# Masked attention and a two-layer MLP on one core: first-layer input sums moved earlier and partly to VectorE, input operands spread over the cycles, leaky ReLU beside attention as a scaled copy and a maximum, weight decoding in halves

## The chip, the core and the metric

The kernel runs on one core of a Trainium2 chip. A core has a matrix engine (TensorE, "PE" in the profile; "PEld" is its weight loading), a vector engine (VectorE, DVE), a scalar engine (ScalarE, ACT), GpSimd (POOL) and a sync engine (SP), which issues the DMAs here. PE results land in PSUM, which DVE and ACT read; everything else lives in SBUF or in DRAM. Every engine works through its own queue in order and waits on semaphores for the others. The metric is the device time in microseconds (us) of one execution; the medians are over three runs.

## The reference, cut to what matters

Attention over 8 batches, 8 heads, 576 positions and 64 columns, with a mask that keeps only scores near the row's maximum, and then a two-layer MLP with a leaky ReLU over all 4608 tokens:

```python
scores = scale * np.matmul(q, k.transpose(0, 1, 3, 2))            # (8, 8, 576, 576)
thresh = np.max(scores, axis=-1, keepdims=True) - tau
scores = np.where(scores >= thresh, scores, -1000000000.0)
attn = np.exp(scores - np.max(scores, axis=-1, keepdims=True))
attn = attn / (np.sum(attn, axis=-1, keepdims=True) + 1e-09)
x = (attn @ v).transpose(0, 2, 1, 3).reshape(4608, 512)
h = x @ w_in                                                      # w_in 512 x 2048
g = np.maximum(h, 0.0) + alpha * np.minimum(h, 0.0)               # one alpha per column
return (g @ w_out).astype(np.float32)                             # w_out 2048 x 512
```

The weights arrive as 64-bit words and are decoded on the chip. Every product keeps its precision by splitting an operand into a rounded high part and the rest ("hi" and "lo": names with h and l) and adding three products.

## The kernel before, in words

**Attention (0 to about 840 us).** The 64 heads are handled in 32 pairs of nine row blocks each: 288 units, one per "cycle" of a written loop that goes on for a few cycles at both ends. In a cycle PE computes the scores of a coming block (`s`, L431) and transposes an earlier block's weights (`t`, L475), DVE takes the row maximum (`nmx`, L446) and applies the mask (`p`, L466), ACT takes the exponential (`p`, L454) and the threshold (`thr`, L459), and both split the transposed weights for the product with v (`av`, L578). Finished tokens go to DRAM as `xs`.

**The MLP beside attention.** Of the 16 blocks of the hidden layer six (`fcs1`) are computed in the plain way, in groups of 256 tokens, beside attention where the loop finds room on PE (class `Mlp`). One "L1 step" is 12 matmuls into `pha` (L218). `step_l1` first reads the group's x back from `xs` (`load_x`, L198), splits it a set number of cycles later (XO; `split_x`, L204 on ACT and L206 on POOL) and lets the first L1 step come two cycles after that. Leaky ReLU follows an L1 step: DVE writes alpha·min(h, 0) (`pta`, L230), ACT writes max(h, 0) (`pra`, L231), POOL adds them (L241), then POOL (or ACT) rounds the sum to `ga` and POOL takes the rest (L247, L248). The second layer (`acca`, L254) comes when all six blocks of the group are there, L2O cycles later at the earliest; HOLD is a stretch of cycles near attention's end in which no L1 step is placed.

**The jobs (about 840 to 930 us).** The last groups of the six blocks run alone as "jobs": `first_layer` (`phj`, L218; leaky ReLU as two DVE instructions, L236 and L237; `gj`, L245 and L248) and `second_layer` (`accj`, L254; its sum leaves through ACT as `poj`, L1089). In between come the weights of the next stage (`w`, `wa`, L866, L869, L995 to L1008).

**Products a (about 930 to 1195 us).** The other ten blocks use seven products in place of eight for a 2 x 2 blocking (a Strassen-Winograd scheme), first for the first layer: six sets of 768 tokens, for each of which four quarters of x (`xr`, loaded by L1131) give seven operands. Four of these are sums: 7 = 11 − 01, 6 = 7 + 00, 4 = 10 − 6 and 5 = 01 − 00 (the digits name the quarters), `tt` at L1136 on DVE for set 0 and at L1139 on POOL, in two halves, for sets 1 to 5. Each operand is split into hi (ACT, L866) and lo (POOL, or DVE for a few of set 0, L869). The products are `pX`, `pW`, `pY` (L1252); ACT copies them out scaled (`c`, L1269, L1277) and DVE joins them (L1280, L1292). PE may start a product on a bank when the copy of the bank's last one is done. `x_at` places every sum, hi and lo of a set at a cycle counted from the product that first needs it (`need`).

**Products b (about 1195 to 1420 us)** do the same for the second layer (L1430), with PE busy throughout.

**Word decoding.** `Split64` turns 512 columns of 64-bit words into floats in seven steps on ACT, DVE and POOL. For the second-stage blocks' first-layer weights this is done early, beside attention (`early_word`, one block every EW = 20 cycles).

**What sets the order.** The instructions of PE, ACT, DVE and POOL stand in the order in which the loop writes them; `at_cycle` puts a step into a cycle. The order of the DMAs on SP's queue is set by a scheduler.

Of the kernel before, what the change touches and what calls it, by code (L numbers as in the profile page):

```python
# [37 lines left out]
HOLD = (-16, -1)  # L38
# [16 lines left out]
XO = 1  # L55
L2O = 3
# [10 lines left out]
EW0, EW = 62, 20  # L67
# [14 lines left out]
def tile_masked_attention_moe(  # L82
# [34 lines left out]
    class Split64:  # L117


        def __init__(self, pool, raw, temp_pool, temp, eng, src, a, name, split=False):  # L120
            self.split = split
            self.pool, self.raw_tag, self.temp_pool, self.temp_tag = pool, raw, temp_pool, temp
            self.eng = [nc.vector if e == 'v' else nc.gpsimd for e in eng]
            self.src, self.a, self.name = src, a, name
# [1409 lines left out]
```

## Time and profile before

| | us |
| --- | --- |
| median of 3 runs (lowest to highest) | 1418.66 (1417.18 to 1421.1) |
| profiled execution | 1421.49 |
| its span, first to last instruction | 1419.6 |
| PE busy (matmuls) | 1320.9, 93% |
| DVE / ACT / POOL busy | 1126.5 (79%) / 967.7 (68%) / 761.7 (54%) |

An engine's busy time is counted over the whole span, so the share is an average over stages with different limits. "Idle before" is the time in which the engine stood still before an instruction or a group of them, and the name behind the arrow is what released it. PEclk is the share of full clock that was granted to PE: 1.0 is 2.4 GHz, 0.5 is 1.2 GHz, and a value between them is a mixture over the stretch.

### The profile page before, as it was taken

The numbers are of one execution on the slowest core, as the hardware profiler recorded it, in microseconds if no ns is written. First come the engines' busy times: TensorE is split into PE (matmuls) and PEld (weight loads), VectorE is DVE, ScalarE is ACT, GpSimd is POOL, SyncE is SP. The second block draws the span as 40 slices with busy tenths as digits, with TensorE's granted clock in tenths as the row PEclk, the third lists the DMA queues.
The fourth block names the chain that finished last, engine by engine and source line by source line (L and its number), as shares of the span: only waits on it lengthen the run. The fifth ranks groups of instructions, "written<-read, shape, count | busy, mean of one in ns | idle before, by whom it ended". The sixth has DMA issues, their size and how long they took to land.

```text
span 1419.6 us, 26277 instructions
## 1 busy us (share of the span) xinstructions
PE 1320.9 (93%) x8998; PEld 1226.8 (86%) x8998; DVE 1126.5 (79%) x2113; ACT 967.7 (68%) x2109; POOL 761.7 (54%) x938
## 2 busy tenths in 40 slices
PE   5998989989989998999999988988899999999998
PEld 4666889989888888998989977978889999999998
DVE  6898898998988988888898874556667558787885
ACT  6887888888878877888888863455656565333332
POOL 3775675774765766676675636646766664000000
PEclk9999999999999999999999999999999999999999
DMA  7655546545555464455545404335444466556542
GB/s 230 168 136 146 148 127 163 153 131 156 148 142 144 127 166 130 132 156 142 160 117 152 119 34 136 103 125 163 160 156 158 134 201 198 179 178 200 182 154 74
DMA packets 146166, 210.32 MB, mean 148 GB/s; under 512 B 16016, under 2 KB 89008, under 8 KB 146032
## 3 DMA queue, kind: packets, MB, share of 16 engines
q1 hardware_dynamic: 146032, 208.63, 50.1%
q8 instruction: 72, 1.18, 0.3%
q14 instruction: 62, 0.51, 0.1%
HBM read 111.75 MB, written 54.67 MB: 117 GB/s over the span
## 4 chain that ended last, share of the span: by engine, by line
PE 56%; issue 11%; DVE 10%; POOL 10%; ACT 8%; DMA 3%; SPq 1%; POOLq 0%; DVEq 0%; ACTq 0%
PE av L578 9%; PE pX L1430 9%; PE s L431 8%; PE acca L254 6%; PE t L475 5%; PE pha L218 5%; PE pW L1430 5%; POOL xl L869 3%; PE pY L1430 2%; DVE p L466 2%; DVE nmx L446 2%; PE pX L1252 2%; POOL xt L1139 2%; PE phj L218 2%; ACT p L454 1%
## 5 line engine op out<-in xcount | busy, mean ns | idle before, releaser
L446 DVE TENSOR_REDUCE nmx<-s 128x1 f32<-128x576 f32 x288 | 216.5, 752 | 66.7 <-PE s L431 62.9
L466 DVE SCALAR_TENSOR_TENSOR p<-s,thr,p 128x576 f32<-128x576 f32 x256 | 206.6, 807 | 3.3 <-ACT thr L459 2.8
L431 PE MATMUL s<-kh,qst 128*128 128x288 f32 x640 | 145.7, 317 | 55.2 <-DVE p L466 36.7
L454 ACT ACTIVATE p<-s,nmx 128x576 f32<-128x576 f32 x256 | 190.1, 742 | 9.1 <-DVE nmx L446 8.8
L431 PEld LDWEIGHTS s<-kh,qst 128*128 128x128 f32 x640 | 100.4, 192 | 86.8 <-issue 43.0
L254 PE MATMUL acca<-wo,ga 128*128 128x512 f32 x504 | 158.4, 426 | 0.0
L475 PE MATMUL t<-ident,p 128*128 128x128 f32 x1024 | 156.4, 276 | 1.1 <-DVE p L466 1.1
L1252 PE MATMUL pX<-xh,wa 128*128 128x384 f32 x480 | 139.6, 347 | 17.4 <-ACT c L1269 12.6
L218 PE MATMUL pha<-xh,wi 128*128 128x256 f32 x688 | 140.5, 287 | 5.9 <-ACT pra L231 4.3
L431 PE MATMUL s<-kl,qst 128*128 128x288 f32 x640 | 133.9, 299 | 0.0
L1430 PE MATMUL pX<-wb,gh 128*128 128x256 f32 x720 | 129.7, 282 | 0.0
L475 PEld LDWEIGHTS t<-ident,p 128*128 128x128 f32 x1024 | 127.5, 142 | 1.5 <-DVE p L466 1.3
L218 PEld LDWEIGHTS pha<-xh,wi 128*128 128x128 f32 x688 | 112.0, 189 | 12.4 <-ACT pra L231 6.9
L1430 PEld LDWEIGHTS pX<-wb,gh 128*128 128x128 f32 x720 | 111.6, 191 | 0.0
L1252 PEld LDWEIGHTS pX<-xh,wa 128*128 128x128 f32 x480 | 90.4, 193 | 23.5 <-ACT c L1269 15.8
L866 ACT ACTIVATE gh<-gr 128x1280 fp32r<-128x1280 f32 x45 | 57.4, 1275 | 74.9 <-PE pX L1430 38.9
L578 PE MATMUL av<-eo,vst 128*128 128x322 f32 (+1 forms) x512 | 107.8, 334 | 0.2 <-ACT xb L591 0.2
L531 DVE TENSOR_TENSOR eo<-t,eo 128x512 fp32r<-128x512 f32 (+1 forms) x168 | 97.2, 591 | 9.8 <-ACT eo L527 9.5
L431 PEld LDWEIGHTS s<-kl,qst 128*128 128x128 f32 x640 | 102.8, 192 | 0.0
L1430 PE MATMUL pX<-wb,gl 128*128 128x256 f32 x360 | 101.6, 282 | 0.0
L254 PEld LDWEIGHTS acca<-wo,ga 128*128 128x128 f32 x504 | 89.5, 194 | 11.4 <-DVE e L531 0.3
L218 PE MATMUL pha<-xl,wi 128*128 128x256 f32 x344 | 97.0, 282 | 0.2 <-POOL xl L206 0.2
(213 smaller groups left out, 3855.3 us busy)
## 6 DMA issues: line engine op xcount, KB each, us to landing
gd<-c SPq DMA_DIRECT2D x90, 192.0 KB
gr<-gd SPq DMA_DIRECT2D x24, 640.0 KB
kr<-in_k_dram SPq DMA_DIRECT2D x31, 320.0 KB
rb<-rvd SPq DMA_DIRECT2D x64, 144.0 KB
xs<-xa SPq DMA_DIRECT2D x32, 288.0 KB
pin<-part SPq DMA_DIRECT2D x18, 512.0 KB
out_dram<-pin SPq DMA_DIRECT2D x18, 512.0 KB
vr<-in_v_dram SPq DMA_DIRECT2D x28, 320.0 KB
```

Source lines behind the costliest of these rows:

```text
L218: nc.tensor.matmul(ph[:, :n], w[:, c, :], xx[:, c, :n], start=(c == 0 and ti == 0), stop=(c == NCC - 1 and ti == 2),)
L254: nc.tensor.matmul(acc[:m, :], gg[:, g, o : o + m], w, start=(first and ti == 0), stop=(last and ti == 2))
L431: nc.tensor.matmul(ps[:, h, :288], w, kk[:, a + h * 288 : a + (h + 1) * 288], start=(ki == 0 and i == 0), stop=(ki == 1 and i == n - 1),)
L446: nc.vector.tensor_reduce(self.nmx[:, j : j + 1], self.S[u][0][:, :, :288], axis=AX.XY, op=ALU.max, negate=True)
L454: nc.scalar.activation(pj, ps[:, :, :288], AF.Exp, bias=nmx[:, j : j + 1], scale=1.0)
L466: nc.vector.scalar_tensor_tensor(pj, ps[:, :, :288], thr[:, j : j + 1], pj, op0=ALU.is_ge, op1=ALU.mult, accum_out=self.sm[:, c : c + 1])
L475: nc.tensor.transpose(tb[:, c, :], pt[:, j, j * D + c * P : j * D + (c + 1) * P], ident)
L531: nc.vector.tensor_tensor(dst[1], ps, f(dst[0]), op=ALU.subtract)
L578: nc.tensor.matmul(pa[:m, :n], w, x, start=(part == 0 and c == 0), stop=(part == z.parts[-1] and c == NKC))
L866: nc.scalar.activation(dst, src, AF.Copy)
L1252: nc.tensor.matmul(ph[:, :H1], a, x[:, c], start=(fresh and c == 0 and ti == 0), stop=(c == 1 and ti == 2), skip_group_check=not fresh,)
L1430: nc.tensor.matmul(acc[:, tb * H2 : (tb + 1) * H2], g[:, pr, tb * P : (tb + 1) * P], w, start=(fresh and n == 0 and ti == 0), stop=(n == l ...
```

## The change

- **Leaky ReLU.** Everywhere two instructions in place of three (beside attention) or of two on DVE (jobs): ACT copies h scaled by a per-column value (`turn_sb`) to `pta`, and DVE takes max(h·`slope_sb`, `pta`). POOL's add and the tile `pra` are gone; the tile `pta` has three buffers (two before). For this form the second-layer weights of the six blocks get the column's factor while they are decoded (`size` with `tiny_sb`, and one more ACT copy of `wto` in `round`).
- **x of the MLP beside attention.** x is loaded into the tile `xl` itself, and lo replaces it there; `xr` is gone. XO goes from 1 to 2, L2O from 3 to 1, HOLD from the last 16 to the last 12 cycles.
- **Early word decoding** in halves of 256 columns, one every 10 cycles.
- **Jobs.** The second layer of the job before the last stands between the last job's fifth and sixth first layers, not behind the sixth. The two `poj` copies of the last job stand between the splits of set 0.
- **Sums of x, sets 1 to 5.** Sums 6 and 5 are single DVE instructions of 768 columns; sums 7 and 4 stay on POOL in halves. Loads, sums, hi and lo have cycles of their own (`need` −33; sums −25, −21, −13, −11; hi at −28, −23, −19, −16, −5, −3, −1, in the order 1, 7, 2, 6, 4, 5, 3; lo a cycle behind).

```diff
-HOLD = (-16, -1)
+HOLD = (-12, -1)
-XO = 1
-L2O = 3
+XO = 2
+L2O = 1
-EW0, EW = 62, 20
+EW0, EW = 62, 10
...
-        def round(self, hi):
+        def round(self, hi, turn=None):
             self.hi = hi
+            if turn is not None:
+                nc.scalar.activation(f(self.t), f(self.t), AF.Copy, scale=turn)
             nc.scalar.activation(hi, f(self.t), AF.Copy)
...
     def load_x(pool, t0, n, gn, bufs):
-        xr = pool.tile([P, NCC, gn], F32, tag=f"xr", name=f"xr{gn}_{t0}", bufs=bufs)
+        xl = pool.tile([P, NCC, gn], F32R, tag="xl", name=f"xl{gn}_{t0}", bufs=bufs)
...
-        nc.scalar.activation(xh[:, :, :n], xr[:, :, :n], AF.Copy)
-        xl = pool.tile([P, NCC, gn], F32R, tag="xl", name=f"xl{gn}_{t0}", bufs=bufs)
-        nc.gpsimd.tensor_tensor(xl[:, :, :n], xr[:, :, :n], f(xh[:, :, :n]), op=ALU.subtract)
+        nc.scalar.activation(xh[:, :, :n], f(xl[:, :, :n]), AF.Copy)
+        nc.gpsimd.tensor_tensor(xl[:, :, :n], f(xl[:, :, :n]), f(xh[:, :, :n]), op=ALU.subtract)
...
-        nc.vector.tensor_scalar(t[:, :n], ph[:, :n], 0.0, alpha_sb[:, fc : fc + 1], op0=ALU.min, op1=ALU.mult)
-        nc.scalar.activation(r[:, :n], ph[:, :n], AF.Relu)
-        return t, r
...
-        nc.vector.tensor_scalar(t[:, :n], ph[:, :n], 0.0, alpha_sb[:, fc : fc + 1], op0=ALU.min, op1=ALU.mult)
-        nc.vector.scalar_tensor_tensor(t[:, :n], ph[:, :n], 0.0, t[:, :n], op0=ALU.max, op1=ALU.add)
+        col = slice(fc, fc + 1)
+        nc.scalar.activation(t[:, :n], ph[:, :n], AF.Copy, scale=turn_sb[:, col])
+        nc.vector.scalar_tensor_tensor(
+            t[:, :n], ph[:, :n], slope_sb[:, col], t[:, :n], op0=ALU.mult, op1=ALU.max
+        )
         return t
-
-    def prelu2(t, r, n):
-        nc.gpsimd.tensor_tensor(t[:, :n], t[:, :n], r[:, :n], op=ALU.add)
...
-                if k == 0 and num > 0 and not last and not (num == 1 and pending.begun):
+                if k == (GB - F1 - 1 if last else 0) and num > 0 and not (num == 1 and pending.begun):
                     second_layer(pending, mem.mp1)
...
-            def tt(out, a, b, op):
-                if first:
+            def tt(out, a, b, op, alone=False):
+                if first or alone:
                     nc.vector.tensor_tensor(out, a, b, op=op)
...
-                tt(st[5], st[0, 1], st[0, 0], op=ALU.subtract)
+                tt(st[5], st[0, 1], st[0, 0], ALU.subtract, True)
...
-                tt(temp(6), st[7], st[0, 0], op=ALU.add)
+                tt(temp(6), st[7], st[0, 0], ALU.add, True)
...
-            at_cycle(need[1] - 32, load)
-            for m, n in enumerate(USE):
-                c = need[1] - 22 + 3 * m
-                if m >= XB - 7:
-                    c = max(c, start[u - 1, USE[m + 7 - XB]] + 2)
-                fn = {7: sub7, 6: add6, 4: sub4, 5: sub5}.get(n)
-                if fn:
-                    at_cycle(c - 1, fn)
-                at_cycle(c, hi, n)
-                at_cycle(c + 1, lo, n)
+            at_cycle(max(i, need[1] - 33), load)
+            for c, fn in ((-25, sub7), (-21, add6), (-13, sub5), (-11, sub4)):
+                at_cycle(need[1] + c, fn)
+            for c, n in zip((-27, -22, -18, -15, -4, -2, 0), USE):
+                at_cycle(need[1] + c - 1, hi, n)
+                at_cycle(need[1] + c, lo, n)
...
-        others()
-        for put in puts:
-            put()
+        others(puts)
```

**ACT in attention, around two leaky ReLUs.** These are rows of ACT's queue in the same stretch of one group (the numbers behind the names count tiles). Before:

```order
L231 ACTIVATE pra_3_6826<-pha_3_6786 128x256
L527 ACTIVATE tt_123<-tk_t 64x64
L527 ACTIVATE tt_125<-tk_t 64x64
L527 ACTIVATE eo_117<-t_4_6815 128x4x64 x2
L454 ACTIVATE p_2_6804<-s_6_6808,nmx_5_6801 128x576
L459 ACTIVATE thr_5_6802<-nmx_5_6801,ntau_sb 128x1
L231 ACTIVATE pra_4_6884<-pha_4_6830 128x256
```

and now:

```order
L522 ACTIVATE tt_125<-tk_t 64x64
L522 ACTIVATE eo_117<-t_4_6777 128x4x64 x2
L449 ACTIVATE p_2_6766<-s_6_6770,nmx_5_6763 128x576
L454 ACTIVATE thr_5_6764<-nmx_5_6763,ntau_sb 128x1
L232 ACTIVATE pta_3_6845<-pha_3_6790,turn_sb 128x256
L522 ACTIVATE eo_117<-t_5_6820 128x4x128
L449 ACTIVATE p_3_6852<-s_7_6811,nmx_7_6849 128x576
```

One ACT instruction per leaky ReLU stands there in both; it reads the L1 step's result and nothing of DVE's now, and the L1 steps (blocks 3, 4) lie on other cycles than before.

**ACT at the hand-over from the jobs to products a.** `xh0_n` is the hi of operand n of set 0, `poj3_0` and `poj3_128` are the last job's copies, `c1_0` and `c7_0` the first products' copies. Before:

```order
L866 ACTIVATE xh0_7_12973<-xt0_7_12841 128x768
L866 ACTIVATE xh0_2_12977<-xr0_10_12839 128x768
L866 ACTIVATE xh0_6_12981<-xt0_6_12848 128x768
L866 ACTIVATE xh0_4_12987<-xt0_4_12985 128x768
L866 ACTIVATE xh0_5_12992<-xr0_01_12836 128x768
L866 ACTIVATE xh0_3_12997<-xr0_11_12833 128x768
L1089 ACTIVATE poj3_0_12941<-accj3_0_12922 128x512
L1089 ACTIVATE poj3_128_12961<-accj3_128_12942 128x512
L1269 ACTIVATE c1_0_13035<-pX0_13011,turn_sb_69 128x384
```

and now:

```order
L861 ACTIVATE xh0_7_12920<-xt0_7_12859 128x768
L1081 ACTIVATE poj3_0_12888<-accj3_0_12869 128x512
L861 ACTIVATE xh0_2_12926<-xr0_10_12857 128x768
L1081 ACTIVATE poj3_128_12908<-accj3_128_12889 128x512
L861 ACTIVATE xh0_6_12932<-xt0_6_12866 128x768
L861 ACTIVATE xh0_4_12938<-xt0_4_12936 128x768
L861 ACTIVATE xh0_5_12943<-xr0_01_12854 128x768
L861 ACTIVATE xh0_3_12948<-xr0_11_12851 128x768
L1256 ACTIVATE c1_0_12982<-pX0_12958,turn_sb_69 128x384
```

The two `poj` copies move ahead of five and of four hi's; `c1_0` stays behind all of them.

**POOL in products a, set 1.** `xt1_n` and `xr1_01` on the left of the arrow at L1139 (now L1131) are sums, `xl1_n` are lo's, `wto` and `wro` are words of coming weights. Before:

```order
L1139 TENSOR_TENSOR xt1_7_13157<-xr1_11_13029,xr1_01_13031 128x384 x2
L847 TENSOR_TENSOR wro6_13018<-wro6_13018 128x512
L869 TENSOR_TENSOR xl1_7_13172<-xt1_7_13157,xh1_7_13171 128x384 x2
L869 TENSOR_TENSOR xl1_2_13209<-xr1_10_13033,xh1_2_13208 128x384 x2
L1139 TENSOR_TENSOR xt1_6_13234<-xt1_7_13157,xr1_00_13027 128x384 x2
L869 TENSOR_TENSOR xl1_6_13247<-xt1_6_13234,xh1_6_13246 128x384 x2
L145 TENSOR_SCALAR wto7_13272<-wto7_13272 128x512
L1139 TENSOR_TENSOR xt1_4_13325<-xr1_10_13033,xt1_6_13234 128x384 x2
L847 TENSOR_TENSOR wro7_13175<-wro7_13175 128x512
L869 TENSOR_TENSOR xl1_4_13340<-xt1_4_13325,xh1_4_13339 128x384 x2
L1139 TENSOR_TENSOR xr1_01_13031<-xr1_01_13031,xr1_00_13027 128x384 x2
L869 TENSOR_TENSOR xl1_5_13370<-xr1_01_13031,xh1_5_13369 128x384 x2
```

and now:

```order
L1131 TENSOR_TENSOR xt1_7_13051<-xr1_11_12967,xr1_01_12969 128x384 x2
L145 TENSOR_SCALAR wto6_13054<-wto6_13054 128x512
L864 TENSOR_TENSOR xl1_7_13077<-xt1_7_13051,xh1_7_13076 128x384 x2
L839 TENSOR_TENSOR wro6_12973<-wro6_12973 128x512
L864 TENSOR_TENSOR xl1_2_13126<-xr1_10_12971,xh1_2_13125 128x384 x2
L864 TENSOR_TENSOR xl1_6_13163<-xt1_6_13102,xh1_6_13162 128x384 x2
L1131 TENSOR_TENSOR xt1_4_13219<-xr1_10_12971,xt1_6_13102 128x384 x2
L145 TENSOR_SCALAR wto7_13222<-wto7_13222 128x512
L839 TENSOR_TENSOR wro7_13129<-wro7_13129 128x512
L864 TENSOR_TENSOR xl1_4_13287<-xt1_4_13219,xh1_4_13286 128x384 x2
L864 TENSOR_TENSOR xl1_5_13315<-xr1_01_12969,xh1_5_13314 128x384 x2
```

Sums 6 and 5 have left POOL's queue. Of sum 6, DVE's queue now has one row, six places ahead of the one that ends the product `pZ1`.

## Rows read from the trace of the kernel before

**Rows 1.** First part of the page, the PE group: busy time, share of the span, instructions, engine by engine.

```profile
PE 1320.9 (93%) x8998; PEld 1226.8 (86%) x8998; DVE 1126.5 (79%) x2113; ACT 967.7 (68%) x2109; POOL 761.7 (54%) x938
```

**Rows 2.** Busy time by stage. The columns are: stretch and its length in us, busy us (and instructions) of PE, PEld, DVE, ACT, POOL, the mean granted clock, the DMA engines' share, GB/s.

```profile
150.00:820.00 670.00, 636.99 (x4539) 596.20 (x4540) 588.81 (x1282) 562.96 (x1336) 443.59 (x541) 0.99 0.51 142
880.00:945.00 65.00, 56.00 (x312) 50.85 (x312) 37.96 (x70) 27.57 (x66) 38.73 (x48) 0.90 0.36 110
945.00:1195.00 250.00, 230.24 (x1277) 223.25 (x1277) 163.10 (x274) 151.63 (x299) 159.76 (x164) 0.98 0.48 156
1195.00:1404.00 209.00, 209.00 (x1755) 209.00 (x1754) 171.20 (x153) 74.07 (x60) 0.91 (x1) 1.00 0.57 179
```

**Rows 3.** What PE waited for between 150 and 820 us: total us, times, longest.

```profile
PE s L431 <- DVE p L466: 22.5, 24, 2.0
PE pha L218 <- ACT pra L231: 4.3, 6, 1.6
```

**Rows 4.** Busy time by stage once more (columns as in rows 2), for the four places with two cycles on end in which PE had no MLP work.

```profile
182.00:192.00 10.00, 6.95 (x52) 6.31 (x51) 8.26 (x17) 9.31 (x20) 7.46 (x8) 1.00 0.63 171
285.00:295.00 10.00, 6.87 (x51) 6.24 (x50) 8.74 (x20) 8.62 (x19) 7.54 (x7) 1.00 0.65 171
390.00:400.00 10.00, 6.87 (x38) 6.11 (x37) 8.32 (x20) 8.04 (x18) 7.02 (x6) 0.83 0.70 180
497.00:508.00 11.00, 8.36 (x39) 7.44 (x40) 7.97 (x18) 7.52 (x17) 7.72 (x7) 0.70 0.81 222
```

**Rows 5.** Timeline of PE, the start of two such cycles: start, us, engine, line, operation, and in brackets the idle time before it and what ended it.

```profile
186.22 0.50 PE L431 MATMUL s<-kh,qst 128*128 128x288 f32 x2 [1.53 <-DVE p L466]
188.94 0.50 PE L431 MATMUL s<-kh,qst 128*128 128x288 f32 x2 [1.52 <-DVE p L466]
```

**Rows 6.** Instructions grouped by line, whole span: count, busy us, mean ns of one, idle time before them with what ended it.

```profile
L230 DVE TENSOR_SCALAR pta<-pha,alpha_sb 128x256 f32<-128x256 f32 x82 | 38.4, 468 | 2.3 <-PE pha L218 1.5
L231 ACT ACTIVATE pra<-pha 128x256 f32<-128x256 f32 x82 | 31.3, 381 | 40.6 <-DVE pta L230 40.3
L241 POOL TENSOR_TENSOR pta<-pta,pra 128x256 f32<-128x256 f32 x82 | 60.6, 739 | 59.4 <-ACT pra L231 59.4
L237 DVE SCALAR_TENSOR_TENSOR ptj<-phj,ptj 128x256 f32<-128x256 f32 x22 | 9.3, 424 | 0.8
L1269 ACT ACTIVATE c<-pX,turn_sb 128x384 f32<-128x384 f32 x60 | 34.7, 578 | 23.2 <-PE pX L1252 23.1
L1277 ACT ACTIVATE c<-pZ 128x384 f32<-128x384 f32 x30 | 14.6, 488 | 5.0 <-DVE pZ L1292 4.7
```

**Rows 7.** Timeline of PE at one L1 step whose bank was not free.

```profile
663.56 0.39 PE L218 MATMUL pha<-xh,wi 128*128 128x256 f32 x1 [1.57 <-ACT pra L231]
```

**Rows 8.** Timelines of PE and ACT at a change of group beside attention: the last matmul of the old group's last L1 step, and the split of the new group's x, which had been loaded at 608 us.

```profile
637.77 0.28 PE L218 MATMUL pha<-xh,wi 128*128 128x256 f32 x1
640.62 1.07 ACT L204 ACTIVATE xh<-xr 128x1024 fp32r<-128x1024 f32 x1
```

**Rows 9.** Timelines of SP (issue of loads) and ACT (first use): in the jobs, and at the hand-over.

```profile
872.28 1.01 SPq L881 DMA_DIRECT2D xrj<-xs  x2
...
875.86 0.42 ACT L888 ACTIVATE xhj<-xrj 128x256 fp32r<-128x256 f32 x1 [4.13 <-DMA xrj<-xs]
...
915.18 4.68 SPq L1131 DMA_DIRECT2D xr<-xs  x6
...
920.73 0.85 ACT L866 ACTIVATE xh<-xr 128x768 fp32r<-128x768 f32 x1 [2.83 <-DMA xr<-xs]
```

**Rows 10.** Grouped by line, whole span: an ACT copy of word decoding with a column as its scale, and the same with a number.

```profile
L142 ACT ACTIVATE wro<-wro,tiny_sb 128x512 f32<-128x512 uint32 x10 | 7.6, 763 | 0.0
L142 ACT ACTIVATE wro<-wro 128x512 f32<-128x512 uint32 x6 | 4.0, 672 | 0.0
```

**Rows 11.** Timelines of DVE and PE in the jobs.

```profile
882.93 0.93 DVE L1008 TENSOR_TENSOR w<-w,sum 128x256 f32<-128x256 f32 x1 [1.29 <-POOL wa L869]
...
884.77 0.58 PE L218 MATMUL phj<-xhj,wi 128*128 128x256 f32 x1 [3.95 <-DVE ptj L237]
```

**Rows 12.** Timelines of PE, DVE and POOL at the hand-over: the 72 matmuls behind the last first layer, a product of set 0, two sums of set 0, and a split on POOL between them.

```profile
915.47 16.56 PE L254 MATMUL accj<-wo,gj 128*128 128x512 f32 x72
...
939.44 0.69 PE L1252 MATMUL pY<-xh,wa 128*128 128x384 f32 x1 [4.86 <-ACT poj L1089]
...
923.13 1.33 DVE L1136 TENSOR_TENSOR xt<-xr,xr 128x768 f32<-128x768 f32 x1 [5.68 <-DMA xr<-xs]
...
923.60 1.45 POOL L869 TENSOR_TENSOR wa<-w,wa 128x256 fp32r<-128x256 f32 x1
...
925.79 0.94 DVE L1136 TENSOR_TENSOR xr<-xr,xr 128x768 f32<-128x768 f32 x1
```

**Rows 13.** What PE and ACT waited for between 945 and 1195 us: total us, times, longest.

```profile
PE pX L1252 <- ACT c L1269: 12.6, 10, 2.3
PE pX L1252 <- DVE pZ L1292: 4.8, 8, 1.9
PE pW L1252 <- ACT c L1269: 2.4, 2, 2.1
...
ACT xh L866 <- POOL xt L1139: 25.7, 10, 3.8
ACT xh L866 <- POOL xr L1139: 13.8, 5, 4.0
```

More of the change, by code (lines that the diff above doesn't have):

```diff
@@ L117, in tile_masked_attention_moe, with __init__ @@
     class Split64:
-        def __init__(self, pool, raw, temp_pool, temp, eng, src, a, name, split=False):
-            self.split = split
+        def __init__(self, pool, raw, temp_pool, temp, eng, src, a, name, split=False, width=DM):
+            self.split, self.width = split, width
             self.pool, self.raw_tag, self.temp_pool, self.temp_tag = pool, raw, temp_pool, temp
@@ L720, in act @@
             def act(ph=ph):
-                if alone:
-                    st[fi] = (prelu(mem.mp1, G1, fcs1[fi], n, ph, name, 2),)
-                    return
-                st[fi] = prelu1(mem.mp1, G1, fcs1[fi], n, ph, name, 2)
-                prelu2(*st[fi], n)
+                st[fi] = prelu(mem.mp1, G1, fcs1[fi], n, ph, name, 3)
             def spl():
                 g = mem.mp1.tile([P, 2, G1], F32R, tag="g", name=f"g{name}", bufs=GB)
-                split_g(g, st.pop(fi)[0], n, None if alone else dict(p=nc.gpsimd, v=nc.vector).get(SPG))
+                split_g(g, st.pop(fi), n, None if alone else dict(p=nc.gpsimd, v=nc.vector).get(SPG))
                 st["g"][fi] = g
@@ L799, in decode_at @@
             at_cycle(load, w.load)
-        at_cycle(c, w.size)
+        col = slice(fc, fc + 1)
+        at_cycle(c, w.size, *((tiny_sb[:, col],) if io == "o" else ()))
         at_cycle(c + 1, w.clamp)
@@ L804, in decode_at @@
         at_cycle(c + 4, w.power)
-        at_cycle(c + 4, lambda: w.round(weight(pool, fc, io)[:, 0]))
+        at_cycle(c + 4, lambda: w.round(weight(pool, fc, io)[:, 0], turn_sb[:, col] if io == "o" else None))
         at_cycle(c + 5, w.rest)
@@ L853, in word_at, with early_word @@
         at_cycle(c + pace[6], done, w)
[L855 removed]
+    def early_word(n, h, c):
         fc = fcs2[n]
[L857 removed]
+        w_, a = DM // 2, NCC // 2
+        src = w_in[h * w_ : (h + 1) * w_, fc * P : (fc + 1) * P].rearrange("(cc p) f -> p cc f", p=P)
+        w = Split64(mem, ("wx", 1), mem, ("wxt", 1), "ppp", src, a, f"i{fc}_{h}", width=w_)
         def done(w):
             nc.gpsimd.tensor_tensor(f(w.t), f(w.t), f(w.low), op=ALU.add)
[L861 removed]
+            nc.sync.dma_start(wid[n][:, h * w_ : (h + 1) * w_], f(w.t))
         word_at(c, w, c - 5, done)
@@ L898, in tile_masked_attention_moe @@
     at_cycle(6, signs)
-    for n_ in range(NJ):
-        early_word(n_, EW0 + EW * n_)
+    for n_ in range(2 * NJ):
+        early_word(n_ // 2, n_ % 2, EW0 + EW * n_)
     with tc.manual_schedule(engines=ENGINES) if ENGINES else ExitStack():
@@ L1068, in first_layer @@
             cycle()
-            t = prelu(mem.mp1, G1, fc, job.n, ph, name, 2)
-            if job is jobs[-1] and j == F1 - 1:
-                job.g[j] = mem.ws.tile([P, 2, G1], F32R, tag="w1", name=f"g{name}", bufs=2)
-            else:
-                job.g[j] = mem.mp1.tile([P, 2, G1], F32R, tag="g", name=f"g{name}", bufs=GB)
+            t = prelu(mem.mp1, G1, fc, job.n, ph, name, 3)
+            job.g[j] = mem.mp1.tile([P, 2, G1], F32R, tag="g", name=f"g{name}", bufs=GB)
             split_g(job.g[j], t, job.n)
@@ L1182, in x_at, with others @@
                 sub5()
-                def others():
+                def others(puts):
                     for n in USE[1:]:
```

25 lines of the change are left out of this document (10 added, 15 removed).

## Prediction

> **What bounds the kernel now.** I read the busy times first: PE is at work for 93% of the span [rows 1], and the change leaves the number of matmuls as it is, so it can only win what PE waits and what PE loses at half clock. Hence the busy times by stage next [rows 2]. From 150 to 820 us PE is busy for 637 of 670 us, and DVE (589) and ACT (563) nearly as much: PE, DVE and ACT share the bound there. From 880 to 945 us PE has 9 us of idle time and a mean clock of 0.90, which is 13 us at 1.2 in place of 2.4 GHz, or 6.5 us of work lost. From 945 to 1195 us PE idles for 20 us. From 1195 us on it never stops, and nothing in the change can help. Then the waits: beside attention PE waits for DVE's masked `p` (22.5 us) and a little for ACT's `pra` (4.3 us) [rows 3]; in products a it waits for ACT's copies (12.6 + 2.4 us) and for DVE (4.8 us), while ACT itself waits 25.7 + 13.8 us for POOL's sums [rows 13]. ACT works in order, so a hi that waits for a sum holds the copies behind it, and PE's next product holds with them. That chain is the largest wait that the change touches.
>
> The sum is made against the profiled execution, 1421.5 us, which lies 2.8 us above the median of 1418.7; the sum's difference is applied to the median.
>
> **1. Leaky ReLU beside attention.** DVE's 82 instructions of 468 ns become 82 of the kind that the jobs have at 424 ns [rows 6]: 82 × 0.044 = 3.6 us off DVE. ACT's relu (381 ns) becomes a copy with a column as scale. No row has it at this size; a copy with such a scale takes 90 ns more than one without (578 against 488) [rows 6], so I estimate 0.47 us, and 82 × 0.09 = 7.4 us more for ACT. What hides it: ACT now stands idle for 40.3 us before these relus, waiting for DVE [rows 6], and the new copy reads only PE's result. POOL loses 60.6 us of adds [rows 6]; no wait of PE names POOL there, so that counts as nothing. The bank `pha` is free after DVE and then ACT now (0.47 + 0.38), and after ACT and then DVE in future (0.47 + 0.42): the chain isn't shorter, but DVE ends it and no longer an instruction that may stand behind others on ACT. An L1 step waited 1.57 us for it at 663.6 us [rows 7], all of them 4.3 us [rows 3]. I take 3 us of that and 2 of DVE's 3.6: **−5 us**. Bounds: −8 (both whole) and +7 (ACT's extra all on the path).
>
> **2. Where the MLP work lies (XO, L2O, HOLD).** Four times there are two cycles on end without MLP work, in which PE waits some 1.5 us for `p` [rows 5]. In those windows PE is busy for 6.95, 6.87, 6.87 and 8.36 us of 10, 10, 10 and 11 [rows 4]. At the stage's mean share of 0.951 [rows 2] it would be 39.0 in all, against 29.05: 9.9 us short. In the last two the clock fell, to 0.83 and 0.70 in the mean [rows 4]: 3.4 + 6.6 us at half, another 5.0 lost. By the written order the second cycle of each pair is filled now (L2O is 1). But the work put there is taken from other cycles, and more of those are only partly filled; a cycle lasts 2.7 us [rows 5] by DVE and ACT whether PE is full or not. So I take a third of the 14.9: **−5 us**, bounds −15 and +3.
>
> **3. x loaded in place.** The load must now wait until PE has done the old group's last L1 step, where it had been issued some 30 us ahead [rows 8]. The split came 2.6 us after that step's end (638.05 to 640.62) [rows 8]; one cycle later by XO makes 5.3 us. From issue to use a load took 3.6 us in the jobs and 5.55 with five others beside it [rows 9]. So the wait is between nothing and 0.3 us for each of some 14 groups. ACT stands at the split if the load is late, and behind it the exponentials and the copies that free PE's banks; on SP, the loads of k and v stand behind the waiting one. I take 0.15 × 14: **+2 us**; bounds 0 and 3 × 14 = +42 (the second rival).
>
> **4. Decoding.** Six second-layer weights get one more ACT copy with a column as scale, 0.76 us by the row of the same size, and six `low` copies cost 0.09 more (763 against 672) [rows 10]: 5.1 us on ACT, before and at the start of the MLP work. The early words in halves move the same columns in more instructions, between other work. **+1.5 us**, bounds 0 and +6.
>
> **5. Jobs.** PE waited 3.95 us at 884.8 us for leaky ReLU on DVE, where a weight sum stood ahead of it and waited for POOL [rows 11]. The clock fell there and at the hand-over, half of the 6.5 us each. Now the splits of the last jobs' x stand one or two first layers earlier on ACT, and DVE has one instruction for a leaky ReLU, not two. I take a bit over half of 3.95 + 3.25: **−4 us**, bounds −7 and +2.
>
> **6. Hand-over.** Between the last first layer and products a lay 72 matmuls, 16.6 us [rows 12]; 36 now, 8.3 us, since the other half moved ahead. x of set 0 was issued at 915.2 us and first used 5.55 us later [rows 9]; its first sum began at 923.1 [rows 12], so 7.9 us after the issue. Counted from the end of the last first layer, the operand 7 is split at 7.9 + 1.3 (sum) + 0.85 (hi) + 0.95 (lo, estimated as a DVE sum of that size) = 11.0, where PE could start on it at 8.3 + 1.4 = 9.7: a new wait of 1.3. The product behind, `pY`, waited 4.86 us for the `poj` copies [rows 12], which now stand ahead of most hi's; that wait goes. But the next, on the bank of `pX0`, needs `c1_0`, still behind all hi's, and hi 4 needs a sum after operand 6: about 17 by the same count, and it would have been 17.7 without the change (941.5 − 915.6 − 8.3). So the wait only moves. With some of the 3.25 us of clock: **−2 us**, bounds −8 and +8.
>
> **7. Sums in products a.** PE's waits are 12.6 + 4.8 + 2.4 = 19.8 us [rows 13], and the mean clock of 0.98 over 250 us [rows 2] makes 5 us more. Sum 6 and its hi are now five cycles apart, sum 5 and its hi ten, so ACT no longer waits there: its 39.5 us [rows 13] mostly go. Some 4 us of PE's waits are of another kind (two at the end, where products b begin). The price is on DVE: ten sums at 0.94 to 1.33 us [rows 12], 9.4 to 13.3 us, in a stage in which it is busy for 163 of 250 us [rows 2]. It stands in DVE's idle time unless a sum falls ahead of the instruction that frees a bank; then PE waits up to 1.33 us. Of 15.8 us of waits and 2 of clock I take **−13 us**; bounds −18 and +5 (nothing gained, every second sum on the path, less the waits that go anyway).
>
> One row speaks against part 7. The sum at 923.13 us took 1.33 us and the one at 925.79 us 0.94; a split on POOL began at 923.60 [rows 12]. That is 0.4 us for a sum that meets POOL, or 4 us in ten, which I have inside the 9.4 to 13.3. The Trainium skill ("SBUF — State Buffer", Who interferes with whom) goes further: a VectorE instruction with two SBUF inputs and a GpSimd instruction that reads SBUF shut each other out for the whole of an instruction. By that rule each sum could wait for a whole split, the 1.45 us of the row; the trace shows 0.4, less than the rule allows.
>
> **Sum:** −5 − 5 + 2 + 1.5 − 4 − 2 − 13 = −25.5 us. 1421.5 − 25.5 = 1396.0 for an execution like the profiled one; 1418.7 − 25.5 = **1393 us** as the median.
>
> **Rivals.**
> - *Attention doesn't gain.* The cycles are bound by DVE and ACT together, the relu and the add were off the path, and the filled pairs are paid for elsewhere. For it: ACT gets 7.4 us more, and 589 and 563 of 670 us busy leave no engine as the single cause [rows 2]. Against it: a third of PE's waits lie in those windows. Parts 1 and 2 at zero: 1403; with part 3 at +5, 1406 us.
> - *Slower: x in place holds ACT.* At each change of group the split waits on a load that couldn't be issued before. For it: no spare buffer, and SP's queue in order ahead of the load. Against: a wait of 3 us needs a load of 8, and the longest of rows 9 is 5.55. 14 × 3 = 42 us: 1393 − 2 + 42 = 1433 us. It decides from 2 us a group on: 14 × 2 = 28 is more than the rest of the sum, 27.5.
> - *The sums on DVE take back their gain.* DVE's joins come late behind a sum that waits for POOL's sum 7 or for its splits: ten times 1.33 us, so part 7 gives nothing: 1406 us; together with the first rival 1419, no change. For it: PE already waits 4.8 us for DVE there [rows 13]. By the rule of the skill above this rival is the stronger one, at 10 × 1.45 us.
> - *The hand-over is exposed.* With half the cover, the 1.3 us at operand 7 becomes 8 if x is late: 1403 us.
>
> **Chances.** The forecast 0.55; attention without gain 0.20; sums without gain 0.09, and together with the former 0.05; x in place 0.07; hand-over 0.04. The likeliest case alone lies between 1381 and 1404 us. The range is 1375 to 1413: below, parts 2 and 7 near their bounds; above, it takes in the single failures. A measurement of this kernel can tell 0.3%, 4.3 us, from no change. Faster than 1414.4 us: 0.85; within: 0.08; slower than 1422.9: 0.07.
>
> **What would show it.** In the profile after: `xh` waits little for sums in products a, and PE there is busy for at least 240 us of the stage (part 7); DVE's sums of 768 columns take 0.95 to 1.4 us; the ACT copy of `pta` takes 0.47 us and PE waits for no `pra` or `pta` (1); no two bare cycles on end, and the clock stays at 1.0 in attention (2); ACT's split of `xl` waits under 0.5 us for its DMA (3); no wait of 4 us in the jobs (5); a wait before `pX0` that stays (6). The forecast is wrong if the split waits 2 us a group, if attention ends no earlier, or if PE's waits for DVE in products a grow by more than 10 us.

## The result and the profile after

The changed kernel took 1432.1 us (median of 7 runs, 1425.6 to 1435.9), the kernel before 1419.1 us (7 runs): a ratio of 1.0085, 95% interval 1.0063 to 1.0107. It is slower. Profiled execution: 1431.8 us, span 1429.6.

PE's marks divide the difference by stage. Timeline of PE before (start, us, engine, line, operation): the last scores of attention, and the first matmul of products b.

```profile
837.52 0.43 PE L431 MATMUL s<-kl,qst 128*128 128x288 f32 x2
...
1184.89 0.28 PE L1430 MATMUL pX<-wb,gh 128*128 128x256 f32 x1
```

The same after, with the first product of products a between them (before it stood at 931.87 us):

```profile
868.12 0.43 PE L426 MATMUL s<-kl,qst 128*128 128x288 f32 x2
...
961.02 0.34 PE L1239 MATMUL pX<-xh,wa 128*128 128x384 f32 x1
...
1194.56 0.40 PE L1417 MATMUL pX<-wb,gh 128*128 128x256 f32 x2
```

Attention ends 30.6 us later; jobs and hand-over take 92.9 us where they took 94.4; products a take 233.5 us, not 253.0, so 19.5 less. 30.6 − 1.5 − 19.5 = 9.6 of the 10.0 us by which the spans differ.

Busy time by stage after (columns as in [rows 2]); the first and the third row answer to the first and the third there, the second to the jobs:

```profile
150.00:850.00 700.00, 642.61 (x4530) 595.38 (x4530) 591.78 (x1314) 576.96 (x1360) 389.22 (x492) 0.99 0.49 135
850.00:960.00 110.00, 101.47 (x660) 91.13 (x660) 56.56 (x114) 63.23 (x161) 59.50 (x77) 1.00 0.32 101
961.00:1195.00 234.00, 225.55 (x1259) 222.69 (x1258) 171.83 (x281) 153.61 (x299) 141.17 (x146) 0.97 0.51 166
```

Beside attention PE, DVE and ACT are all *less* busy by share than before, although ACT has some 8 us more to do (39.3 us of copies in place of 31.3 us of relus): all of them wait more. What for, between 150 and 850 us (who waited for whom: total us, times, longest; PE's rows answer to [rows 3]):

```profile
PE s L426 <- DVE p L461: 43.0, 55, 2.3
PE s L426 <- issue: 10.7, 4, 2.8
PE pha L219 <- DVE pta L233: 1.7, 4, 0.6
...
ACT p L449 <- DVE nmx L441: 36.8, 60, 1.9
...
DVE nmx L441 <- PE s L426: 48.7, 82, 2.0
DVE pta L233 <- ACT pta L232: 37.0, 50, 1.9
```

And ACT's wait for the row maximum before (150 to 820 us):

```profile
ACT p L454 <- DVE nmx L446: 3.9, 5, 1.6
```

The last row of the first list is new. Before, ACT's relu waited 40.3 us for DVE [rows 6]; now DVE's maximum waits 37.0 us for ACT's copy (42.7 us over the whole span). PE waits 43.0 us for DVE's `p` where it had waited 22.5, and ACT 36.8 us for `nmx` where it had waited 3.9. The groups by line (columns as in [rows 6]) show that the copy costs the 0.47 us that were expected. The maximum takes 482 ns, not the 424 of the jobs' instruction of before, so DVE's work is no shorter than with the 468 ns of [rows 6]:

```profile
L233 DVE SCALAR_TENSOR_TENSOR pta<-pha,slope_sb,pta 128x256 f32<-128x256 f32 x84 | 40.5, 482 | 43.4 <-ACT pta L232 42.7
L232 ACT ACTIVATE pta<-pha,turn_sb 128x256 f32<-128x256 f32 x84 | 39.3, 468 | 2.4 <-PE pha L219 2.4
...
L206 ACT ACTIVATE xh<-xl 128x1024 fp32r<-128x1024 f32 x15 | 15.8, 1054 | 4.1 <-DMA xl<-xs 4.0
L861 ACT ACTIVATE xh<-xt 128x768 fp32r<-128x768 f32 x18 | 15.2, 846 | 10.0 <-POOL xt L1131 5.0 <-DVE xt L1128 5.0
```

One such wait from end to end, in the timeline of ACT, DVE and PE:

```profile
496.35 0.69 ACT L378 ACTIVATE qr<-qr 128x576 f32<-128x576 f32 x1
...
496.95 0.42 ACT L141 ACTIVATE wti<-wri 128x256 f32<-128x256 f32 x1
...
497.27 0.42 ACT L142 ACTIVATE wri<-wri 128x256 f32<-128x256 uint32 x1
...
497.59 0.46 ACT L232 ACTIVATE pta<-pha,turn_sb 128x256 f32<-128x256 f32 x1
...
498.08 0.48 DVE L233 SCALAR_TENSOR_TENSOR pta<-pha,slope_sb,pta 128x256 f32<-128x256 f32 x1 [1.90 <-ACT pta L232]
498.48 0.75 DVE L441 TENSOR_REDUCE nmx<-s 128x1 f32<-128x576 f32 x1
499.15 0.81 DVE L461 SCALAR_TENSOR_TENSOR p<-s,thr,p 128x576 f32<-128x576 f32 x1
499.27 0.74 ACT L449 ACTIVATE p<-s,nmx 128x576 f32<-128x576 f32 x1 [0.73 <-DVE nmx L441]
...
500.11 0.50 PE L426 MATMUL s<-kh,qst 128*128 128x288 f32 x2 [2.21 <-DVE p L461]
```

ACT is late with the copy because it first prepares q and decodes a word. DVE stands for 1.90 us, and behind the maximum stand the row maximum and the mask; the exponential waits for the one, PE's next scores for the other.

The hand-over after (timelines of SP, DVE and PE, answering to [rows 9, 12]; the last first layer ended at 953.0 us):

```profile
953.37 3.26 SPq L1123 DMA_DIRECT2D xr<-xs  x6
...
960.85 1.15 DVE L1128 TENSOR_TENSOR xt<-xr,xr 128x768 f32<-128x768 f32 x1 [6.77 <-DMA xr<-xs]
...
962.93 0.44 PE L1239 MATMUL pW<-xh,wa 128*128 128x384 f32 x1 [0.70 <-ACT xh L861]
964.79 0.44 PE L1239 MATMUL pW<-xl,wa 128*128 128x384 f32 x1 [1.41 <-DVE xl L864]
970.20 0.69 PE L1239 MATMUL pX<-xh,wa 128*128 128x384 f32 x1 [2.48 <-ACT c L1256]
```

And the waits in products a, 961 to 1195 us, answering to [rows 13]:

```profile
PE pX L1239 <- ACT c L1256: 2.5, 1, 2.5
PE pW L1239 <- ACT c L1256: 2.0, 1, 2.0
PE pX L1239 <- DVE pZ L1279: 1.8, 3, 0.8
...
ACT xh L861 <- POOL xt L1131: 5.0, 5, 1.6
ACT xh L861 <- DVE xt L1128: 5.0, 2, 2.9
```

ACT's 39.5 us of waits for sums are 10.0, of which the 5.0 for DVE belong to set 0. PE's 19.8 us are 3.8 (the 2.0 and 1.8 of the list). Another 4.6 us in this window (2.48, 1.41 and 0.70, the three rows above) belong to the hand-over, which the window of [rows 13] leaves out.

### The profile page after: what moved, and what is told of

It reads as the page before. It is cut to its first block, busy times and chain, and to the rows that moved or that the text cites. A ratio compares the mean times of both kernels' runs of the same rounds, so it can differ in the third digit from the quotient of the medians.

```text
span 1429.6 us, 26323 instructions
## 1 busy us (share of the span) xinstructions
PE 1320.5 (92%) x8998; PEld 1224.3 (86%) x8998; DVE 1126.8 (79%) x2127; ACT 997.1 (70%) x2162; POOL 686.6 (48%) x865
## 5 line engine op out<-in xcount | busy, mean ns | idle before, releaser
L426 PE MATMUL s<-kh,qst 128*128 128x288 f32 x640 | 149.2, 323 | 86.6 <-DVE p L461 57.9
L249 PE MATMUL acca<-wo,ga 128*128 128x512 f32 x504 | 147.3, 414 | 1.2 <-POOL ga L243 1.2
L1239 PE MATMUL pX<-xh,wa 128*128 128x384 f32 x480 | 136.1, 343 | 6.4 <-DVE pZ L1279 3.9
L861 ACT ACTIVATE gh<-gr 128x1280 fp32r<-128x1280 f32 x45 | 57.4, 1275 | 71.4 <-PE pX L1417 42.7
```

Of the source, the lines that this page charges most:

```text
L249: nc.tensor.matmul(acc[:m, :], gg[:, g, o : o + m], w, start=(first and ti == 0), stop=(last and ti == 2))
L426: nc.tensor.matmul(ps[:, h, :288], w, kk[:, a + h * 288 : a + (h + 1) * 288], start=(ki == 0 and i == 0), stop=(ki == 1 and i == n - 1),)
L861: nc.scalar.activation(dst, src, AF.Copy)
L1239: nc.tensor.matmul(ph[:, :H1], a, x[:, c], start=(fresh and c == 0 and ti == 0), stop=(c == 1 and ti == 2), skip_group_check=not fresh,)
```

## The experiments

Theory A: the maximum's wait for ACT's copy costs the 30 us. Rivals: the new placement of the MLP work (B), the halved words (C), the new form only together with one of these (D). Names that begin with e are edits of the changed kernel, with b of the kernel before. Ratios are to the kernel before, timed on the same chip. All alphas here are below 1, so that the column `turn_sb` is 1.

**The leaky ReLU undone, and done alone.** In e1_relu:

```diff
-                st[fi] = prelu(mem.mp1, G1, fcs1[fi], n, ph, name, 3)
...
+                t, r = prelu1(mem.mp1, G1, fcs1[fi], n, ph, name, 2)
+                prelu2(t, r, n)
```

> The changed kernel with the leaky ReLU beside attention as before (DVE min times alpha, ACT relu, POOL add); all else as changed. Theory A (the maximum on DVE now waits for ACT's copy, 37 us of DVE's time beside attention in the changed kernel's trace, where before DVE read PE's result at once and ACT did the waiting): attention ends 15 to 30 us sooner than the changed kernel's 868 us, time 1403 to 1417 us. Rival B (the placement of the MLP work by XO, L2O and HOLD costs the 30 us): attention ends within 5 us of 868, time 1427 to 1437. Rival C (the early words in halves cost it): as B.

Measured: 1401.3 us, ratio 0.9867 (0.9833 to 0.9901), attention's last scores at 837.2 us. b1_relu is the opposite, the new form put into the kernel before:

> The kernel before with only the leaky ReLU beside attention in the new form (ACT copy, then the maximum on DVE; three buffers for pta, no pra); all else as before. Theory A (each of the 82 leaky ReLUs makes DVE wait for ACT's copy, on DVE's own bound): DVE waits some 35 us for the copy, attention ends 25 to 38 us later than before's 838 us, time 1443 to 1456. Rival D (the new form costs only together with the new placement or the halved words): attention within 8 us of 838, time up to 1426.

Measured: 1451.3 us, ratio 1.0228 (1.0202 to 1.0254), last scores at 865.1 us, and the same new row of waits (150 to 850 us):

```profile
DVE pta L231 <- ACT pta L230: 42.3, 52, 2.4
```

Both ways the new form costs 30 us, with either placement and either way of decoding. Rival D falls.

**The placement and the words.** e2_place sets XO, L2O and HOLD back, e3_words decodes whole words again.

> The changed kernel with XO, L2O and HOLD at their values of before (1, 3, -16); all else as changed, x still loaded in place. Theory A: time within 6 us of the changed kernel's 1432, attention still ends near 868 us; x split a cycle earlier may wait for its load, up to 3 us more a group. Rival B: attention ends near 845 us and the time falls to about 1410. Rival C: no change.

> The changed kernel with the early words whole again (512 columns, one every 20 cycles); all else as changed. Theory A: 10 fewer instruction groups on ACT, DVE and POOL, worth 2 to 6 us: 1426 to 1430. Rival C (the halves cost most of the 30 us): 1405 to 1415. Rival B: as A.

Measured: e2_place 1445.8 us (1.0182, 1.0146 to 1.0218), e3_words 1432.7 us (1.0082, 1.0056 to 1.0107). B and C fall. The halves cost nothing that can be told. The old placement with x loaded in place is even slower, and ACT stands for its loads (150 to 860 us):

```profile
ACT xh L206 <- DMA xl<-xs: 11.1, 5, 3.1
```

**What of the new form costs it.** e4_late keeps every instruction and moves the maximum behind `nmx` on DVE; e13_late_imm takes the column scale from e4_late's copy as well.

```diff
-                st[fi] = prelu(mem.mp1, G1, fcs1[fi], n, ph, name, 3)
+                t = st[fi] = prelu_a(mem.mp1, G1, fcs1[fi], n, ph, name, 3)
+                late = lambda: prelu_b(t, fcs1[fi], n, ph)
...
+                    tail.setdefault(i + ACTO, []).append(late)
```

> The changed kernel with the same instructions, but beside attention DVE's maximum stands at the end of its cycle, behind the row maximum nmx, and no longer ahead of it; ACT's copy stays where it is. Theory A: DVE's wait for ACT's copy falls from 37 us to under 10, ACT's wait for nmx (37 us) falls with it, attention ends 10 to 25 us sooner, time 1407 to 1422. Rivals B and C: DVE's wait is slack, time stays within 4 us of 1432.

> The kernel of e4_late (the maximum behind nmx on DVE) with ACT's copy of h without the column as its scale (the column is 1 for the alphas here, so the value is the same): ACT saves 84 times 0.09 = 7.5 us. If what e4_late leaves over e1_relu (15 us) is ACT's longer instruction: 1408 to 1411. If it is the place of the maximum on DVE, which delays the next mask: 1414 to 1417.

Measured: e4_late 1416.1 us (0.9979, 0.9960 to 0.9999), e13_late_imm 1415.3 us (0.9966, 0.9954 to 0.9979). Order alone is worth some 15 us (the ratio falls from 1.0085 to 0.9979); the 90 ns of the column are worth nothing that can be told. In e4_late DVE no longer waits for the copy, but more for the scores, and PE waits 4.4 us for a bank that the late maximum holds (150 to 850 us):

```profile
DVE nmx L447 <- PE s L432: 71.6, 125, 2.0
...
DVE pta L235 <- ACT pta L231: 2.9, 7, 0.9
...
PE pha L219 <- DVE pta L235: 4.4, 9, 0.6
```

e17_next puts the maximum one cycle later, ahead of `nmx`, and takes it from the copy in SBUF, which frees the bank early:

```diff
-                st[fi] = prelu(mem.mp1, G1, fcs1[fi], n, ph, name, 3)
...
+                nc.scalar.activation(t[:, :n], ph[:, :n], AF.Copy, scale=turn_sb[:, col])
...
+                    nc.vector.scalar_tensor_tensor(
+                        t[:, :n], t[:, :n], alpha_sb[:, col], t[:, :n], op0=ALU.mult, op1=ALU.max
+                    )
...
+            at_cycle(i + SPLO, late)
```

> The changed kernel with the maximum beside attention one cycle later, ahead of nmx as in the changed kernel, taken from ACT's copy alone (max(alpha t, t) with t in SBUF). If all of the 30 us is DVE standing for ACT's copy in a place where DVE has no slack: DVE waits under 5 us for the copy, attention ends at 835 to 842 us, time 1399 to 1406, as e1_relu. If the place of ACT's copy or its length matters: 1410 to 1418, as e4_late.

Measured: 1397.9 us (0.9847, 0.9822 to 0.9871), last scores at 837.0 us: all 30 us are back with an ACT copy and a DVE maximum per leaky ReLU. Groups by line, the copy and the maximum, which waits for nothing (80 of the 84; the last four keep the old place):

```profile
L732 DVE SCALAR_TENSOR_TENSOR pta<-pta,alpha_sb 128x256 f32<-128x256 f32 x80 | 42.7, 534 | 0.0
...
L721 ACT ACTIVATE pta<-pha,turn_sb 128x256 f32<-128x256 f32 x80 | 37.6, 470 | 0.9 <-PE pha L219 0.9
```

e21_late_sbuf and e22_same_sbuf free the bank in the same way, but keep the place of e4_late and of the changed kernel (the jobs' maximum reads SBUF too in these two):

> The kernel of e4_late (the maximum behind nmx) with the maximum taken from ACT's copy in SBUF, so that pha's bank is free after the copy. If e4_late's remaining 15 us came from the held bank: 1398 to 1404. If they came from the place (the maximum no longer fills DVE's wait for the scores and delays the next mask): 1411 to 1418, with DVE still waiting some 70 us for PE's scores.

> The changed kernel with the maximum taken from ACT's copy in SBUF, in its own place ahead of nmx, in the same cycle. If DVE's wait for the copy is the cause: no gain, 1427 to 1437, with 35 us or more of DVE waiting for the copy. If the held bank was: 1400 to 1415.

Measured: 1438.1 us (1.0130, 1.0091 to 1.0169) and 1471.9 us (1.0371, 1.0337 to 1.0404), slower than either expectation. e22_same_sbuf still waits 37.5 us for the copy, so an early bank doesn't help there. But in both the maximum itself took longer, 818 and 866 ns in the mean against 482, and the timeline of e22_same_sbuf shows one such case (the last section has the count):

```profile
309.47 1.44 POOL L388 TENSOR_TENSOR qt<-qr,qst 128x576 fp32r<-128x576 f32 x1 [1.30 <-ACT qr L378]
309.79 1.40 DVE L233 SCALAR_TENSOR_TENSOR pta<-pta,alpha_sb 128x256 f32<-128x256 f32 x1 [0.84 <-ACT pta L232]
```

With both inputs in SBUF it met a POOL instruction and ended 0.3 us after that one. 84 × 0.38 = 32 us more on DVE, which is most of the 40 us against the changed kernel. So e21_late_sbuf doesn't tell whether e4_late's remaining 15 us lie in the held bank or in the place.

e18_pool takes the maximum off DVE altogether (ACT's copy, then two POOL instructions):

> The changed kernel with the leaky ReLU beside attention as ACT's copy and two POOL instructions (t plus (alpha-1) times min(t, 0)); DVE takes no part. If DVE is what bounds the cycles with an L1 step: 80 times up to 0.48 us off it, attention ends at 805 to 830 us, time 1370 to 1395. If PE and ACT bound them as well: 835 to 842 us and 1399 to 1406. POOL gets 84 times 1.15 us, about 97 us in 840.

Measured: 1401.7 us (0.9873, 0.9839 to 0.9907), no faster than e17_next, which keeps the work on DVE. What cost 30 us was DVE's waiting, not the 40 us of DVE work. Whether less DVE work would pay by itself stays open: POOL is busy for 539 of the 680 us from 150 to 830 us here, against 392 in e17_next, and may take the gain back.

From the starts of all `nmx` between the 49th and the 279th of these traces, the mean distance from one to the next, with and without a leaky ReLU on DVE between them:

| kernel | with (80 or 81) | without (150 or 151) |
| --- | --- | --- |
| before | 3.02 us | 2.87 us |
| changed | 3.50 | 2.81 |
| e1_relu | 3.03 | 2.86 |
| b1_relu | 3.48 | 2.81 |
| e4_late | 3.16 | 2.91 |
| e17_next | 2.94 | 2.89 |

80 × 0.48 = 38 us longer with one, 151 × 0.06 = 9 us shorter without: the 30 us lie in the cycles with a leaky ReLU.

**Loading in place and the placement, each by itself.** All four are on the base of e1_relu; e14_best to e16_own also leave out the six ACT copies in the rounding and keep the sums on POOL.

> The kernel of e1_relu (old leaky ReLU beside attention) with XO, L2O and HOLD of before as well (1, 3, -16); x is still loaded in place. If the new placement is worth the 5 us forecast, 1406; if it is worth nothing, 1401; if splitting x one cycle after its load (XO 1) makes ACT wait for the load, as its 11 us of waits in e2_place say, 1410 to 1420.

> The kernel of e12_poolsums without the six extra ACT copies and the column scale's use in the rounding of the second-layer weights (the column is 1 here): the fastest so far less the cost of those copies. If they delay the first cycles (cycles 45 to 63 were 5 us longer in the changed kernel): 1393 to 1396. If they are hidden: 1397 to 1400.

> The kernel of e14_best with x in a buffer of its own again, XO, L2O and HOLD as changed (2, 1, -12). If loading in place costs anything at XO 2 (ACT waited 4 us for it in the changed kernel): 2 to 5 us faster than e14_best; if not, the same.

> The kernel of e14_best with x in a buffer of its own again and XO, L2O and HOLD of before (1, 3, -16). If the placement is worth nothing by itself and XO 2 only pays for loading x in place: within 3 us of e14_best. If the new placement gains: 3 to 8 us slower than e14_best.

Measured: e7_relu_place 1412.1 us (0.9940, 0.9919 to 0.9961), e14_best 1397.6 (0.9846, 0.9829 to 0.9862), e16_own 1397.7 (0.9848, 0.9833 to 0.9864), e15_place_own 1394.1 (0.9821, 0.9804 to 0.9838). With XO at 2, loading in place costs nothing (e14_best against e16_own). The new placement with x in a buffer of its own is 3.6 us slower than the old one (e16_own against e15_place_own; neither branch of the expectation, and the intervals overlap). With x in place the old placement, XO at 1, costs 10.8 us instead (e7_relu_place against e1_relu, ACT waiting 10.9 us for the load), so there loading in place costs some 14 us, an estimate from these two differences.

**The sums in products a.** b2_products puts only the new cycles and the two sums on DVE into the kernel before; e12_poolsums is e1_relu with these sums on POOL:

```diff
-                tt(st[5], st[0, 1], st[0, 0], ALU.subtract, True)
+                tt(st[5], st[0, 1], st[0, 0], ALU.subtract)
...
-                tt(temp(6), st[7], st[0, 0], ALU.add, True)
+                tt(temp(6), st[7], st[0, 0], ALU.add)
```

> The kernel before with only the new cycles of x sums, hi and lo in products a and the sums 6 and 5 of sets 1 to 5 on DVE; attention, jobs and hand-over as before. If spreading the operands is worth the same alone: products a shorten from 253 us to 233 to 237, time 1400 to 1405, attention's end unchanged at 838. If the gain needs the earlier hand-over: 1406 to 1414.

> The kernel of e1_relu with the sums 6 and 5 of x sets 1 to 5 back on POOL in halves, at their new, early cycles. If the early cycles alone took ACT's waits away (spreading): products a last 239 to 243 us as in e1_relu, time 1401 to 1404. If the move to DVE is what did it (POOL too full): products a last 248 us or more, time 1408 to 1418.

Measured: b2_products 1398.3 us (0.9852, 0.9831 to 0.9874), the whole gain of the changed products a alone. e12_poolsums 1398.2 us (0.9849, 0.9828 to 0.9871), as fast as with the sums on DVE. Groups by line before, and then in e12_poolsums: POOL's sums are no shorter, and ACT's wait for them is as small as with DVE.

```profile
L1139 POOL TENSOR_TENSOR xt<-xt,xr 128x384 f32<-128x384 f32 x10 | 11.0, 1122 | 0.0
...
L866 ACT ACTIVATE xh<-xt 128x768 fp32r<-128x768 f32 x18 | 15.2, 845 | 28.0 <-POOL xt L1139 25.7 <-DVE xt L1136 2.2
```

```profile
L1146 POOL TENSOR_TENSOR xt<-xt,xr 128x384 f32<-128x384 f32 x10 | 11.2, 1142 | 0.0
...
L876 ACT ACTIVATE xh<-xt 128x768 fp32r<-128x768 f32 x18 | 15.2, 847 | 11.3 <-POOL xt L1146 6.3 <-DVE xt L1143 5.0
```

So the cycles did it and not the engine.

**The fastest.** e19_pool_own and e20_next_own put the leaky ReLU of e18_pool and of e17_next on the base of e15_place_own.

> The kernel of e15_place_own with the leaky ReLU of e18_pool: 1394 less what e18_pool gains over e1_relu; 1365 to 1390 if DVE bounds, 1392 to 1397 if not.

> The kernel of e15_place_own with the leaky ReLU of e17_next: 1391 to 1397 if the place on DVE was all; above 1400 if ACT's copy costs more than its relu.

Measured: e19_pool_own 1402.2 us (0.9878, 0.9852 to 0.9904), slower than either expectation, and the cause stays open; e20_next_own 1390.2 us (0.9794, 0.9765 to 0.9823), just under its range and the lowest median of all: 28 us under the kernel before and 42 under the changed one (the interval overlaps that of e15_place_own). It has e17_next's leaky ReLU, the spread operands with all sums on POOL, the jobs and the halved words as changed, and the placement and x's own buffer as before.

## Why the prediction was wrong, point by point

**1, leaky ReLU: wrong, and it alone turned the sign.** Forecast −5 us, measured +30 (e1_relu, b1_relu). The step that failed is "the chain isn't shorter, but DVE ends it": it weighed the length of the chain PE, first reader, second reader, and not on which engine its wait falls. ACT's 40.3 us of idle time before its relu was read as cover for a longer copy. It was where the first reader's delay was absorbed. With the order reversed, the delay of ACT's queue (q, words, exponentials) fell on DVE, behind which stand `nmx` and `p`, the two for which ACT and PE wait. The bound of +7 counted ACT's extra work and no wait; what was queued behind the new wait was never named. Two smaller terms: PE's wait for the bank did fall, from 4.3 to 1.7 us, as forecast; the 2 us taken from DVE did not come, since the maximum took 482 ns and not 424. The copy was right (0.47 us forecast, 0.468 measured).

**2, placement: wrong by some 9 us.** Forecast −5; 3.6 us slower in e16_own against e15_place_own. The bare cycles came singly, as read from the order, but with longer waits (four of up to 2.8 us, 10.7 us in all, put down to issue), and the mean clock beside attention stayed at 0.99.

**3, x in place: right, and its rival fell.** Forecast +2 us; ACT waited 4.0 us in all, and nothing can be told in the time. That the rival's 1433 us lies next to the measured 1432 is chance: those 4.0 us are a tenth of its 42. The rival's mechanism is real in the old placement: with XO at 1 loading in place costs some 14 us.

**4, decoding: right in kind.** Forecast +1.5; the six copies and the halves can't be told from nothing (e12_poolsums to e14_best, e3_words).

**5, jobs: the number came out once, the mechanism is not shown.** Forecast −4. In the changed kernel the wait of 3.95 us is gone and the clock stays at 1.00 from 850 to 960 us. Jobs and hand-over are 1.5 us shorter although two L1 steps (24 matmuls at 0.12 us) moved there: 4.4 us like for like. But e15_place_own has the jobs as changed with the placement of before, and there the wait is back, behind the same weight sum as in [rows 11] (DVE and PE):

```profile
880.08 0.93 DVE L1019 TENSOR_TENSOR w<-w,sum 128x256 f32<-128x256 f32 x1 [1.29 <-POOL wa L880]
...
881.46 0.39 PE L220 MATMUL phj<-xhj,wi 128*128 128x256 f32 x1 [3.99 <-DVE ptj L244]
```

From its last scores to its first product it takes 94.5 us, like the kernel before (94.4). In e2_place, also with the old placement, PE waits 2.7 us there. So the wait went with the new placement, not with the shorter leaky ReLU and the earlier splits of the forecast. e1_relu, which has both the new jobs and the new placement, took 95.8 us at a mean clock of 0.98: even the changed kernel's 92.9 us are in part luck.

**6, hand-over: right in its working.** The new waits at operand 7 are 0.70 + 1.41 us (forecast 1.3), and `pX` goes on 17.2 us after the last first layer (forecast about 17), after a wait of 2.48 us. Together that is 4.6 us where `pY` had waited 4.86: the wait only moved, as worked out, and the −2 us can't be seen.

**7, products a: right by mechanism, mis-sized.** Forecast −13, measured −19.5, and −20.2 alone (b2_products). I held 4 us to be of another kind, and took a share of the rest; in fact PE's waits fell by 16 us, from 19.8 to 3.8. The other 3 us are not explained here. The price feared on DVE didn't come: PE's waits for DVE fell from 4.8 to 1.8 us. The ten sums on DVE took 0.95 to 1.69 us, longer than the 1.4 that were to show it, and 13.3 us in all, the upper end of the forecast. The two that overlapped no POOL instruction took 0.95 us, the other eight 1.11 us and more; this is the longest:

```profile
1066.65 1.69 DVE L1128 TENSOR_TENSOR xr<-xr,xr 128x768 f32<-128x768 f32 x1
```

The rule of the Trainium skill ("SBUF — State Buffer", Who interferes with whom), that a VectorE instruction with two SBUF inputs contends with a GpSimd instruction that reads SBUF, agrees with these durations, but the sums did the time no harm. In e22_same_sbuf it did: there DVE waited until POOL's instruction had ended, as the rule says.

With +30 in place of −5 and −19.5 in place of −13, the forecast's sum would have been +3; with part 2 at +3.6 as well, +12. Measured are +13 us of the medians and 10.0 of the profiled spans.

## What to carry to other kernels

When a change makes one engine's instruction depend on another's, look at what stands behind the waiting instruction, not at how long the chain is: the delay of the first engine's whole queue goes to the second, and it should fall on the engine whose next instructions nobody waits for. Placing the dependent instruction a cycle later hid the delay here (e17_next), with the three buffers of `pta` that the changed kernel already had. Idle time of an engine before an instruction can be the place where a delay is absorbed at hardly any cost (e1_relu, in which ACT waits there, can't be told from e17_next, in which nobody does), and is then no room for more.

## What the runs showed of the hardware that was not expected

The maximum of 128x256 took 482 ns in the mean with one input in PSUM and one in SBUF. With both in SBUF it took 534 ns in e17_next, but 818 and 866 ns in e21_late_sbuf and e22_same_sbuf, up to 1.73 us for one. Its shortest, median and longest time in ns, in the changed kernel and in e22_same_sbuf:

```profile
L233 DVE SCALAR_TENSOR_TENSOR pta<-pha,slope_sb,pta x84: 464/484/486, 168.8 to 882.0; 128x256 f32<-128x256 f32 x84
```

```profile
L233 DVE SCALAR_TENSOR_TENSOR pta<-pta,alpha_sb x84: 467/644/1731, 167.1 to 917.5; 128x256 f32<-128x256 f32 x84
```

What differs is whether POOL is at work at that point of the cycle. In e22_same_sbuf the 31 that overlapped no POOL instruction took 467 to 488 ns, and all 44 that took over 600 ns overlapped one; most of these ended 0.28 us after it. In the changed kernel, with h read from PSUM, 54 of the 84 overlapped a POOL instruction, and none took over 486 ns. So the place in the order also decides how long the instruction takes, and one operand in PSUM kept it from this.
